# Half of the sigmoids written into PSUM rooms that are taken by need, products shared four to four between VectorE and GpSimd

## Chip, core and metric

The program runs on one core of a Trainium2 chip. The metric is the device time of one execution in microseconds (us). Engines are named as in the profile: PE is TensorE, PEld its weight loads, DVE is VectorE, ACT is ScalarE, POOL is GpSimd, SP issues DMAs.

## The reference

Two layers of attention through 32 inducing points are followed by a feed-forward layer whose activation is a rational function. `h`, which has 49920 rows of 2048 elements, is where the work lies.

```python
def mab(q, kv):
    s = scale * (q @ kv.transpose(0, 2, 1))
    s = s - s.max(-1, keepdims=True)
    a = np.exp(s)
    a /= a.sum(-1, keepdims=True) + 1e-09
    return a @ kv
h = mab(I, x)                       # I: 32 inducing points, x: 4 x 12480 x 128
x = mab(x, h).reshape(49920, 128)
...
h = x @ w_in                        # 49920 x 2048
P = a[0] + a[1]*h + a[2]*h**2 + a[3]*h**3
Q = 1.0 + abs(b[0])*abs(h) + abs(b[1])*h**2
out = (P / (Q + 1e-6)) @ w_out
```

## The kernel before

**Tiling.** The tokens of the four batches are cut into 104 blocks of 480 tokens (26 for each batch). A block has eight *units*, numbered 0 to 7; a unit is 256 of the 2048 hidden columns, held as a tile of 128 partitions x 960 elements. In tile names the three numbers are batch, block and unit (`u1_6_0`). All large instructions come from one recording helper, so that all of them stand on line 157; they are told apart by their tiles.

**A unit's way.** `h` after shifting and scaling is called y here. The rational function is written as a linear part, which one extra matmul adds, and a product of a sum with an inverse; the inverse comes from a logarithm and a sigmoid.

- *first*: two matmuls (PE, `hp<-at,st`) put y into a PSUM tile of two banks, called a *room*. There are three rooms (pool `ps_h`), used in turn as a ring: the room of unit i goes to unit i+3 when the *D* of unit i has read it.
- even units: *mask* (DVE, `u<-hp`) writes |y| into an SBUF tile `u`; *pre* (POOL, `l<-u,all`) writes a scaled copy into the SBUF tile `l`; *D* (DVE, `l<-hp,all,l`) multiplies by y in PSUM. Odd units: *abs* (ACT, `u<-hp,all`) writes `u`; *D* (DVE, `l<-u,all,hp`) follows directly.
- *Ln* (ACT, `u<-u`, 1920 elements, two neighbouring units, called a *pair*) and *sigmoid* (ACT, `u<-u,all`, 1920 elements) turn `u` into the inverse, in place. They lie in different table sets: four pairs of Ln, a table load, four pairs of sigmoid, a table load, and so on.
- the last product, out of `l` and the inverse in `u`: units 0, 1, 3, 5, 7 take it on DVE in one instruction (*Ev*, `l<-l,all,u`, both inputs in SBUF), units 2, 4, 6 on POOL in two (*add*, `l<-l,all`, and *Eg*, `l<-l,u`).
- *second*: four matmul passes (PE, `po<-l,w_out`) add the unit into the block's output in the one `po` bank. After unit 7 *fetch* (DVE, `oT<-po`) copies it out, and a DMA stores it.

**Order.** Each engine executes its instructions in the order in which the program was written. Class `Flow` writes it: it keeps a clock for PE, DVE, ACT and POOL, offers every instruction whose inputs are planned (`options`), takes the one that could start first (ties go by `RANK`, for the attention's own work by `GEN`), books its cost from `COST` and writes it (`do`). The attention work of later blocks and batches is mixed in as generators. The plan has locks: an Ev is not planned to begin while POOL has a product's step running, nor POOL's steps while an Ev runs (`lock_v`, `lock_g`).

SBUF tiles `u` come in 7 pairs (`ROOMS`), tiles `l` in 14 (`SLOTS`). Before the main loop (up to about 87 us of the trace) the first batch's inducing attention and the weights are prepared. A second branch of the program (`general`) is not taken with these inputs.

Of the kernel before, what the change touches and what calls it, by code (L numbers as in the profile page):

```python
# [179 lines left out]
class Flow:  # L180
# [3 lines left out]
    COST = {"first": 0.85, "second": 1.4, "linear": 0.35, "fetch": 0.6, "D": 1.13, "mask": 1.08, "Ev": 1.06, "abs": 0.97, "ln": 1.72, "sig": 1.83, "load": 1.28, "pre": 1.1, "add": 1.15, "Eg": 2.22}  # L184
    BATCH = 4
    ON_POOL = (2, 4, 6)
    ROOMS = 7
    SLOTS = 14
    RANK = {"first": 0, "second": 2, "fetch": 0, "D": 0, "mask": 4, "Ev": -1, "abs": 0, "wide": 1, "pre": 1, "add": 3, "Eg": 2, "load": 1}
    GEN = {"pe": 4, "v": 0, "a": 0, "g": 4, "x": 1}  # L190

    def __init__(self, k, units):
        self.k, self.units = k, units
        self.T = dict.fromkeys(("pe", "v", "a", "g"), 0.0)
        self.now, self.sp = 0.0, 0.0
# [1 line left out]
        self.table, self.nl, self.ns, self.stop = "ln", 0, 0, 0
        self.i1 = self.i2 = self.fetched = 0
        self.masks = self.pres = self.abss = 0
        self.ds, self.es = [], []  # L200
# [39 lines left out]

    def options(self):

        us, LAT, C = self.units, self.LAT, self.COST
        for t in self.turns:
            kind, cost = t.need
            if kind in self.T:
                yield kind, max(t.ready, self.lock_v) if kind == "g" else t.ready, self.GEN[kind], cost, ("turn", t)
            elif kind == "x" and self.table == "ln":
                yield "a", t.ready, self.GEN["x"], cost, ("turn", t)
        if self.i1 < len(us):  # L250
            u, old = us[self.i1], us[self.i1 - 3] if self.i1 >= 3 else None
# [8 lines left out]
        if self.full is not None:  # L260
            yield "v", self.full[1] + LAT, self.RANK["fetch"], C["fetch"], ("fetch", None)
        for u in self.ds:
            s = self.slot_at(u.p)
            if s is not None:
                yield "v", max(u.t["d"], s), self.RANK["D"], C["D"], ("D", u)
        if self.masks < self.pairs:
            u = us[2 * self.masks]
            r = self.room_at(self.masks)
            if "first" in u.t and r is not None:
                yield "v", max(u.t["first"] + LAT, r), self.RANK["mask"], C["mask"], ("mask", u)  # L270
        if self.pres < self.masks:
            u = us[2 * self.pres]
            s = self.slot_at(self.pres)
            if s is not None:
                yield "g", max(u.t["mask"] + LAT, s, self.lock_v), self.RANK["pre"], C["pre"], ("pre", u)
        if self.abss < self.pairs:
            u = us[2 * self.abss + 1]
            r = self.room_at(self.abss)
            if "first" in u.t and r is not None:
                yield "a", max(u.t["first"] + LAT, r), self.RANK["abs"], C["abs"], ("abs", u)  # L280
        for u in [u for u in self.es if not u.pool][:1]:
            yield "v", max(u.t["e"], self.lock_g), self.RANK["Ev"], C["Ev"], ("Ev", u)
        for u in [u for u in self.es if u.pool and self.half is None][:1]:
            yield "g", max(u.t["e"], self.lock_v), self.RANK["add"], C["add"], ("add", u)
        if self.half is not None:
            yield "g", self.lock_v, self.RANK["Eg"], C["Eg"], ("Eg", self.half)
        top = self.stop + self.BATCH
        if self.table == "ln":
            if self.nl < min(top, self.pairs):
                a, b = us[2 * self.nl], us[2 * self.nl + 1]  # L290
                if "D" in b.t and "pre" in a.t and "mask" in a.t:
                    yield "a", max(b.t["D"], a.t["pre"]) + LAT, self.RANK["wide"], C["ln"], ("ln", self.nl)
            elif self.ns < self.pairs:
                yield "a", 0.0, self.RANK["load"], C["load"], ("load", "sig")
# [5 lines left out]
    def room_at(self, p):  # L300

        if p in self.room:
            return 0.0
        if p != len(self.room):
            return None
        if p < self.ROOMS:
            return 0.0
        a, b = self.units[2 * (p - self.ROOMS):][:2]
        return max(a.t["E"], b.t["E"]) + self.LAT if "E" in a.t and "E" in b.t else None

    def slot_at(self, p):

        if p in self.slot:
            return 0.0
        q = 2 * p - self.SLOTS
        if p != len(self.slot):
            return None
        if q < 0:
            return 0.0
        a, b = self.units[q:q + 2]  # L320
        return b.t["second"] + self.LAT if "second" in b.t else None
# [8 lines left out]
    def sums(self, p):  # L330
        k, us = self.k, self.units
        if p not in self.slot:
            self.slot[p] = True
            for u in us[2 * p:2 * p + 2]:
                u.g = k.mp.tile([P, 2, BT], F32, tag="l", name=f"l{u.i}", bufs=self.SLOTS)

    def do(self, what, u, start, end):
# [4 lines left out]
        if what == "turn":  # L342
            u.ready = end + LAT
            if u.need[0] == "g":
                self.lock_g = end
# [3 lines left out]
            return  # L349
        if what == "first":  # L350
            k.first(u)
            u.t["first"] = end + 0.1
# [11 lines left out]
        elif what == "mask":  # L364
            self.pair(self.masks)
            V.tensor_scalar(out=u.u.bitcast(I32), in0=u.h.bitcast(I32), scalar1=0x7FFFFFFF, scalar2=None, op0=ALU.bitwise_and)
            u.t["mask"] = end
            self.masks += 1
        elif what == "pre":
            self.sums(self.pres)  # L370
            G.tensor_scalar(out=u.g, in0=u.u, scalar1=1.0, scalar2=p.k1, op0=ALU.mult, op1=ALU.add)
# [4 lines left out]
        elif what == "abs":
            self.pair(self.abss)
            A.activation(u.u, u.h, AF.Abs, bias=p.back, scale=1.0)
            u.t["d"] = end + LAT
            u.p = self.abss  # L380
            self.ds.append(u)
            self.abss += 1
        elif what == "D":
            if u.key[2] % 2:
                self.sums(u.p)
                V.scalar_tensor_tensor(out=u.g, in0=u.u, scalar=p.k1, in1=u.h, op0=ALU.add, op1=ALU.mult)
            else:
                V.scalar_tensor_tensor(out=u.g, in0=u.h, scalar=p.k2, in1=u.g, op0=ALU.add, op1=ALU.mult)
            u.t["D"] = end
            self.ds.remove(u)  # L390
        elif what == "load":
# [4 lines left out]
        elif what == "ln":
            w = us[2 * u]
            A.activation(w.pair, w.pair, AF.Ln, bias=LAM, scale=LAM)
            self.nl += 1
        elif what == "sig":  # L400
            w = us[2 * u]
            A.activation(w.pair, w.pair, AF.Sigmoid, bias=p.lnc, scale=-2.0)
            for w in us[2 * u:2 * u + 2]:
# [676 lines left out]
```

## Time and profile before

| what | us |
| --- | --- |
| median of 3 runs | 2802.0 (2797.62 to 2804.08) |
| profiled execution, its own time | 2795.03 |
| span of the profiled execution, first to last instruction | 2793.1 |
| busy in the span: DVE / PE / ACT / POOL | 2503.2 / 2275.5 / 2221.1 / 1860.7 |

A row of groups gives the line, engine, operation, the tile written and the tiles read, the shape, the count, then busy time and mean duration of one, then the idle time of the engine just before these instructions and what ended it. "x3" in a timeline stands for three instructions that follow one another, with their common time. Instructions of one engine overlap a little at their ends, so that a run of them takes less than their number times the mean of one.

### The profile page before, as it was taken

The page shows a single profiled execution, that of the slowest core. Times are in us where ns is not written, and L with a number is a line of the kernel's source. Part 1 is how long each engine was busy: PE and PEld are TensorE (multiplying, and loading weights), DVE is VectorE, ACT ScalarE, POOL GpSimd, SP SyncE. Part 2 cuts the span into 40 slices and gives each one's busy share as a digit, 9 for nine tenths or more (in the row PEclk, how much of TensorE's full clock was granted, in tenths as well). Part 3 has the DMA queues.
Part 4 walks back from the last instruction along what each step waited for, and adds up shares of the span by engine and source line. Part 5 has one row for each costly group of instructions (what it writes and reads, how often), then busy time and mean ns, then how long its engine had stood idle before and what let it go on. Part 6 is the DMA issues. An engine that isn't in the chain of part 4 may idle for free.

```text
span 2793.1 us, 23849 instructions
## 1 busy us (share of the span) xinstructions
PE 2275.5 (81%) x7516; PEld 1206.6 (43%) x7516; DVE 2503.2 (90%) x2430; ACT 2221.1 (80%) x1561; POOL 1860.7 (67%) x1212
## 2 busy tenths in 40 slices
PE   5887888887978878878877888878897878777787
PEld 2543444443544434444444444444454444343343
DVE  6688999999899898989999999898999999998996
ACT  1577898887878789877788888888788888778885
POOL 2366667677666676766676766666677767666675
PEclk6689999898989999988999999989999999888898
DMA  8222212111012112211012121221110110000000
GB/s 258 70 58 66 56 44 54 43 53 39 15 60 71 53 39 61 60 26 56 25 43 67 46 59 38 60 54 36 46 32 22 32 39 18 27 20 18 22 14 12
DMA packets 117359, 133.68 MB, mean 48 GB/s; under 512 B 13544, under 2 KB 115816, under 8 KB 117224
## 3 DMA queue, kind: packets, MB, share of 16 engines
q1 hardware_dynamic: 117224, 132.06, 16.8%
q8 instruction: 63, 1.03, 0.2%
q14 instruction: 72, 0.59, 0.1%
HBM read 80.89 MB, written 25.56 MB: 38 GB/s over the span
## 4 chain that ended last, share of the span: by engine, by line
DVE 31%; PE 20%; issue 8%; POOL 4%; ACT 4%; DMA 0%; SPq 0%; DVEq 0%; ACTq 0%; POOLq 0%
DVE l L157 24%; PE po L157 16%; DVE u L157 5%; POOL l L157 4%; PE hp L157 4%; ACT u L157 3%; DVE oT L157 1%; ACT L157 1%; PE pd L157 0%; DVE asm L157 0%; DVE st L157 0%; DMA at<-hl 0%; DVE amx L157 0%; DVE hl L157 0%; DVE gs L157 0%
## 5 line engine op out<-in xcount | busy, mean ns | idle before, releaser
L157 PE MATMUL po<-l,w_out 128*128 128x480 f32 x3328 | 1573.8, 618 | 145.1 <-DVE oT L157 79.0
L157 PEld LDWEIGHTS po<-l,w_out 128*128 128x128 f32 x3328 | 676.2, 208 | 827.4 <-issue 580.7
L157 POOL TENSOR_SCALAR l<-u,all 128x960 f32<-128x960 f32 x416 | 540.3, 1300 | 641.9 <-DVE u L157 538.8
L157 DVE SCALAR_TENSOR_TENSOR l<-l,all,u 128x960 f32<-128x960 f32 x520 | 875.4, 1731 | 14.7 <-ACT u L157 14.4
L157 PE MATMUL hp<-at,st 128*128 128x480 f32 x1664 | 620.9, 478 | 317.1 <-DVE l L157 312.8
L157 POOL TENSOR_TENSOR l<-l,u 128x960 f32<-128x960 f32 x312 | 791.5, 2537 | 125.7 <-ACT u L157 112.3
L157 ACT ACTIVATE u<-u 128x1920 f32<-128x1920 f32 x416 | 733.4, 1799 | 163.2 <-DVE l L157 91.1
L157 ACT ACTIVATE u<-u,all 128x1920 f32<-128x1920 f32 x416 | 769.8, 1891 | 1.0
L157 ACT ACTIVATE u<-hp,all 128x960 f32<-128x960 f32 x416 | 434.6, 1054 | 280.5 <-PE hp L157 247.2
L157 DVE TENSOR_SCALAR u<-hp 128x960 int32<-128x960 int32 x416 | 473.5, 1149 | 115.7 <-PE hp L157 111.1
L157 PEld LDWEIGHTS hp<-at,st 128*128 128x128 f32 x1664 | 308.7, 204 | 580.5 <-issue 300.8
L157 DVE SCALAR_TENSOR_TENSOR l<-u,all,hp 128x960 f32<-128x960 f32 x416 | 495.7, 1203 | 28.9 <-ACT u L157 28.4
L157 DVE SCALAR_TENSOR_TENSOR l<-hp,all,l 128x960 f32<-128x960 f32 x416 | 497.8, 1207 | 24.6 <-POOL l L157 23.7
L157 POOL TENSOR_SCALAR l<-l,all 128x960 f32<-128x960 f32 x312 | 465.6, 1492 | 0.2
L157 ACT ACT_TABLE_LOAD x209 | 268.1, 1283 | 4.4 <-PEq L1073 0.7
L157 PEld LDWEIGHTS pd<-HT,xTb 128*120 128x120 f32 x832 | 105.0, 197 | 17.2 <-issue 14.0
L157 PE MATMUL pd<-HT,xTb 128*120 128x32 f32 x832 | 100.9, 274 | 2.3 <-issue 1.9
L157 DVE COPY oT<-po 128x480 f32<-128x480 f32 x104 | 67.5, 649 | 34.4 <-PE po L157 34.4
L157 PE MATMUL po<-at,st 128*128 128x480 f32 x104 | 78.5, 755 | 0.0
L157 POOL MEMSET x<- 120x4 f32 x104 | 10.5, 113 | 62.9 <-PE ph L157 54.5
L157 PE MATMUL ph<-x,eT 120*32 120x129 f32 x832 | 41.3, 335 | 13.2 <-DMA x<-x_t 10.5
L157 POOL TENSOR_TENSOR st<-gs,st 64x512 fp32r<-64x512 f32 x16 | 20.4, 1277 | 32.8 <-ACT st L157 22.4
(87 smaller groups left out, 595.1 us busy)
## 6 DMA issues: line engine op xcount, KB each, us to landing
x<-x_t SPq DMA_DIRECT2D x104, 240.0 KB, 4.1
xTb<-x_c SPq DMA_DIRECT2D x104, 240.0 KB, 2.9
at<-hl SPq DMA_DIRECT2D x416, 60.0 KB, 2.0
out<-oT SPq DMA_DIRECT2D x104, 240.0 KB, 2.0
xTa<-x_c SPq DMA_DIRECT2D x78, 240.0 KB, 2.9
xTw<-x_c SPq DMA_DIRECT2D x5, 960.0 KB, 11.8
raw<-w_in SPq DMA_DIRECT2D x4, 480.0 KB, 14.0
raw<-w_out SPq DMA_DIRECT2D x5, 384.0 KB, 7.0
```

The costliest lines, as they stand in the source:

```text
L157: ins = call(*args, **kw)
```

## The change

The sigmoid is no longer taken by pairs. Units 0, 2, 4, 6 are now those of DVE: their sigmoid (`sigp`, ACT, 960 elements) is written into a PSUM room, tile `i`, and Ev reads it there (`l<-l,all,i`). Units 1, 3, 5, 7 are those of POOL: their sigmoid (`sig`, ACT, 960 elements) stays in place in `u`, and add and Eg follow on POOL. Which units are masked on DVE (0, 2, 4, 6) and which go through abs on ACT (1, 3, 5, 7) stays as it was.

The three rooms have tags of their own (`hp0` to `hp2`). A first or a sigp takes the room that is free earliest in the plan and holds it until its D or Ev. `u` and `l` are now claimed when the first is planned. The plan's locks are gone, and `RANK`, `GEN` and some of `COST` have other numbers. The dictionary lookups `room_at`, `slot_at`, `pair` and `sums` are replaced by `roomy`, `room` and `slot`, which say the same of `u` and `l` unit by unit; `general_unit` and `misc` name their rooms by tag.

```diff
-    COST = {..., "Ev": 1.06, "abs": 0.97, "ln": 1.72, "sig": 1.83, "load": 1.28, "pre": 1.1, "add": 1.15, "Eg": 2.22}
+    COST = {..., "Ev": 1.13, "abs": 0.97, "ln": 1.72, "sig": 1.83, "half": 0.96, "load": 1.28, "pre": 1.1, "add": 1.13, "Eg": 2.22}
+    RANK = {"first": 1, "second": 2, "fetch": 0, "D": 1, "mask": 2, "Ev": 0, "abs": 1, "wide": 2, "sig": 0, "pre": 0, "add": 2, "Eg": 1, "load": 1}
+    GEN = {"pe": 1, "v": 3, "a": 1, "g": 1, "x": 1}
     BATCH = 4
-    ON_POOL = (2, 4, 6)
     ROOMS = 7
     SLOTS = 14
-    RANK = {"first": 0, "second": 2, "fetch": 0, "D": 0, "mask": 4, "Ev": -1, "abs": 0, "wide": 1, "pre": 1, "add": 3, "Eg": 2, "load": 1}
-    GEN = {"pe": 4, "v": 0, "a": 0, "g": 4, "x": 1}
+    BANKS = 3
+    MASKED = (0, 2, 4, 6)
+    ON_POOL = (1, 3, 5, 7)
...
+    def bank(self):
+        free = [t for t in self.banks if t is not None]
+        return min(free) if free else None
+
+    def take(self):
+        i = self.banks.index(self.bank())
+        self.banks[i] = None
+        return i
...
-        if self.i1 < len(us):
-            u, old = us[self.i1], us[self.i1 - 3] if self.i1 >= 3 else None
+        bank = self.bank()
+        if self.i1 < len(us) and bank is not None and self.roomy(us[self.i1]):
+            u = us[self.i1]
...
-        for u in [u for u in self.es if not u.pool][:1]:
-            yield "v", max(u.t["e"], self.lock_g), self.RANK["Ev"], C["Ev"], ("Ev", u)
+        for u in self.ev[:1]:
+            yield "v", u.t["e"], R["Ev"], C["Ev"], ("Ev", u)
...
-        elif self.ns < self.nl:
-            yield "a", 0.0, self.RANK["wide"], C["sig"], ("sig", self.ns)
+        elif self.sigs:
+            for u in [u for u in self.sigs if u.pool][:1]:
+                if u.n % 2 == 0 and us[u.n + 1].pool:
+                    yield "a", 0.0, R["wide"], C["sig"], ("sig2", u)
+                else:
+                    yield "a", 0.0, R["wide"], C["half"], ("sig", u)
+            for u in [u for u in self.sigs if not u.pool][:1]:
+                if bank is not None:
+                    yield "a", bank, R["sig"], C["half"], ("sigp", u)
...
         elif what == "sig":
-            w = us[2 * u]
-            A.activation(w.pair, w.pair, AF.Sigmoid, bias=p.lnc, scale=-2.0)
+            A.activation(u.u, u.u, AF.Sigmoid, bias=p.lnc, scale=-2.0)
+            u.t["e"] = end + LAT
+            self.sigs.remove(u)
+            self.eg.append(u)
+        elif what == "sigp":
+            u.bank = self.take()
+            u.inv = k.hp(u, "i")
+            A.activation(u.inv, u.u, AF.Sigmoid, bias=p.lnc, scale=-2.0)
+            u.t["e"], u.t["left"] = end + LAT, end
+            self.sigs.remove(u)
+            self.ev.append(u)
         elif what == "Ev":
-            V.scalar_tensor_tensor(out=u.g, in0=u.g, scalar=p.k3, in1=u.u, op0=ALU.add, op1=ALU.mult)
-            u.t["E"] = self.lock_v = end
-            self.es.remove(u)
+            V.scalar_tensor_tensor(out=u.g, in0=u.g, scalar=p.k3, in1=u.inv, op0=ALU.add, op1=ALU.mult)
+            u.t["E"] = end
+            self.banks[u.bank] = end + LAT
+            self.ev.remove(u)
...
+    def hp(self, u, name):
+        return self.ps_h.tile([P, 2, 512], F32, tag=f"hp{u.bank}", name=f"{name}{u.i}", bufs=1)[:, :, 0:BT]
```

ACT's queue from the table load ahead of the sigmoids of block 5 (batch 1) to the last of these sigmoids, before; `u1_6_x` are the abs of the block that follows:

```order
L157 ACT_TABLE_LOAD
L157 ACTIVATE u1_5_0_4827<-u1_5_0_4827,all_202 128x1920
L157 ACTIVATE u1_6_2_4972<-hp1_6_3_4974,all_202 128x960 [waits PE_49]
L157 ACTIVATE u1_5_2_4843<-u1_5_2_4843,all_202 128x1920
L157 ACTIVATE u1_6_4_5008<-hp1_6_5_4991,all_202 128x960 [waits PE_49,Pool_49]
L157 ACTIVATE u1_5_4_4898<-u1_5_4_4898,all_202 128x1920
L157 ACTIVATE u1_5_6_4923<-u1_5_6_4923,all_202 128x1920 [waits Activation_49]
```

The same place after the change; `i1_5_x` are the sigmoids into PSUM rooms:

```order
L157 ACT_TABLE_LOAD
L157 ACTIVATE i1_5_0_5252<-u1_5_0_5084,all_202 128x2x480 [waits DVE_49,PE_49]
L157 ACTIVATE u1_6_0_5216<-h1_6_1_5234,all_202 128x960 [waits PE_49]
L157 ACTIVATE u1_5_0_5084<-u1_5_0_5084,all_202 128x960
L157 ACTIVATE u1_5_2_5111<-u1_5_2_5111,all_202 128x960
L157 ACTIVATE u1_6_2_5242<-h1_6_3_5262,all_202 128x960 [waits PE_49]
L157 ACTIVATE u1_5_4_5157<-u1_5_4_5157,all_202 128x960 [waits Activation_49]
L157 ACTIVATE u1_5_6_5198<-u1_5_6_5198,all_202 128x960 [waits Activation_49]
L157 ACTIVATE i1_5_2_5301<-u1_5_2_5111,all_202 128x2x480 [waits DVE_49]
L157 ACTIVATE u1_6_4_5274<-h1_6_5_5282,all_202 128x960 [waits PE_49,Pool_49]
L157 ACTIVATE i1_5_4_5310<-u1_5_4_5157,all_202 128x2x480 [waits DVE_49]
L157 ACTIVATE i1_5_6_5315<-u1_5_6_5198,all_202 128x2x480 [waits DVE_49]
```

Four instructions of 1920 elements have become eight of 960. The sigmoids into `i` each wait for DVE, which none of the sigmoids did before. The abs of unit 1 of block 6, which stood ahead of this table load, now stands behind it.

DVE's queue at the same place, from the first product of block 5 on, before:

```order
L157 SCALAR_TENSOR_TENSOR l1_5_0_4833<-l1_5_0_4833,all_202,u1_5_0_4827 128x960 [waits Activation_49]
L157 SCALAR_TENSOR_TENSOR l1_5_1_4834<-l1_5_1_4834,all_202,u1_5_0_4827 128x960
L157 SCALAR_TENSOR_TENSOR l1_5_3_4850<-l1_5_3_4850,all_202,u1_5_2_4843 128x960 [waits Activation_49]
L157 SCALAR_TENSOR_TENSOR l1_6_3_4979<-u1_6_2_4972,all_202,hp1_6_3_4974 128x960 [waits PE_49]
L157 TENSOR_SCALAR e2_4361,mxs2_4362<-pc2_4_4994 128x240 [waits PE_49]
L157 SCALAR_TENSOR_TENSOR l1_6_5_5023<-u1_6_4_5008,all_202,hp1_6_5_4991 128x960 [waits Activation_49]
L157 TENSOR_SCALAR e2_4361,mxs2_4362<-pc2_4_4994 128x240
L157 TENSOR_SCALAR u1_6_4_5008<-hp1_6_4_4984 128x960 [waits DVE_49]
L157 TENSOR_SCALAR u1_6_6_5034<-hp1_6_6_5025 128x960 [waits DVE_49,PE_49]
L157 SCALAR_TENSOR_TENSOR l1_5_5_4908<-l1_5_5_4908,all_202,u1_5_4_4898 128x960 [waits Activation_49]
L157 SCALAR_TENSOR_TENSOR l1_5_7_4936<-l1_5_7_4936,all_202,u1_5_6_4923 128x960 [waits Activation_49]
```

And after the change:

```order
L157 SCALAR_TENSOR_TENSOR l1_5_0_5085<-l1_5_0_5085,all_202,i1_5_0_5252 128x960 [waits Activation_49]
L157 COPY oT1_4_5258<-po1_4_0_5175 128x480 [waits DMAHW7_49,PE_49]
L157 SCALAR_TENSOR_TENSOR l1_6_2_5243<-h1_6_2_5244,all_202,l1_6_2_5243 128x960 [waits Pool_49]
L157 SCALAR_TENSOR_TENSOR l1_6_1_5233<-u1_6_0_5216,all_202,h1_6_1_5234 128x960 [waits DVE_49,Activation_49]
L157 SCALAR_TENSOR_TENSOR l1_6_3_5261<-u1_6_2_5242,all_202,h1_6_3_5262 128x960 [waits Activation_49]
L157 TENSOR_SCALAR u1_6_4_5274<-h1_6_4_5276 128x960 [waits PE_49]
L157 SCALAR_TENSOR_TENSOR l1_5_2_5112<-l1_5_2_5112,all_202,i1_5_2_5301 128x960 [waits Activation_49]
L157 SCALAR_TENSOR_TENSOR l1_6_4_5275<-h1_6_4_5276,all_202,l1_6_4_5275 128x960 [waits Pool_49]
L157 SCALAR_TENSOR_TENSOR l1_6_5_5281<-u1_6_4_5274,all_202,h1_6_5_5282 128x960 [waits Activation_49]
L157 SCALAR_TENSOR_TENSOR l1_5_4_5158<-l1_5_4_5158,all_202,i1_5_4_5310 128x960 [waits Activation_49]
L157 SCALAR_TENSOR_TENSOR l1_5_6_5199<-l1_5_6_5199,all_202,i1_5_6_5315 128x960 [waits Activation_49]
```

Five products with two SBUF inputs have become four with one input in PSUM. Between the first and the second of them now stand a fetch, three D and a mask of block 6.

## Rows read from the trace of the kernel before

**Rows 1.** Part 1 of the page: busy us of each engine in the whole span, share, instructions.

```profile
PE 2275.5 (81%) x7516; PEld 1206.6 (43%) x7516; DVE 2503.2 (90%) x2430; ACT 2221.1 (80%) x1561; POOL 1860.7 (67%) x1212
```

**Rows 2.** Busy time of each engine in the stretch from 200 to 2600 us, past the start and ahead of the end.

```profile
core 0: us, PE busy (x) PEld busy (x) DVE busy (x) ACT busy (x) POOL busy (x), PEclk, DMA share, GB/s
200.00:2600.00 2400.00, 1978.94 (x6497) 1054.42 (x6497) 2203.99 (x2000) 1987.52 (x1389) 1655.02 (x1055) 0.91 0.16 43
```

**Rows 3.** Groups of DVE in the same stretch: Ev, the two kinds of D, mask.

```profile
L157 DVE SCALAR_TENSOR_TENSOR l<-l,all,u 128x960 f32<-128x960 f32 x467 | 786.2, 1731 | 9.5 <-ACT u L157 9.2
L157 DVE SCALAR_TENSOR_TENSOR l<-hp,all,l 128x960 f32<-128x960 f32 x373 | 446.3, 1206 | 22.1 <-POOL l L157 21.3
L157 DVE SCALAR_TENSOR_TENSOR l<-u,all,hp 128x960 f32<-128x960 f32 x373 | 444.3, 1203 | 25.1 <-ACT u L157 24.8
L157 DVE TENSOR_SCALAR u<-hp 128x960 int32<-128x960 int32 x374 | 425.6, 1149 | 95.9 <-PE hp L157 91.6 <-issue 1.8 <-POOL l L157 1.2
```

**Rows 4.** Groups of ACT in the same stretch: sigmoid, Ln, abs, table loads.

```profile
L157 ACT ACTIVATE u<-u,all 128x1920 f32<-128x1920 f32 x376 | 696.0, 1891 | 0.9
L157 ACT ACTIVATE u<-u 128x1920 f32<-128x1920 f32 x372 | 655.8, 1799 | 132.8 <-DVE l L157 81.2 <-POOL l L157 44.4 <-DVE asm L157 6.0
L157 ACT ACTIVATE u<-hp,all 128x960 f32<-128x960 f32 x374 | 390.7, 1054 | 258.1 <-PE hp L157 229.9 <-issue 20.5 <-POOL l L157 3.9
L157 ACT ACT_TABLE_LOAD x188 | 241.2, 1283 | 3.3
```

**Rows 5.** Groups of POOL in the same stretch: Eg, pre, add.

```profile
L157 POOL TENSOR_TENSOR l<-l,u 128x960 f32<-128x960 f32 x281 | 709.0, 2523 | 111.0 <-ACT u L157 99.2
L157 POOL TENSOR_SCALAR l<-u,all 128x960 f32<-128x960 f32 x373 | 486.9, 1307 | 560.7 <-DVE u L157 480.3 <-PE po L157 50.3 <-PE hp L157 8.1
L157 POOL TENSOR_SCALAR l<-l,all 128x960 f32<-128x960 f32 x281 | 419.9, 1494 | 0.2
```

**Rows 6.** Least, median and greatest duration in ns over the whole span, of the instructions that write or read the tiles `l` (Ev, the D, pre, add, Eg) and `po`.

```profile
L157 DVE SCALAR_TENSOR_TENSOR l<-l,all,u x520: 1196/1260/3253, 125.3 to 2772.8; 128x960 f32<-128x960 f32 x174
L157 POOL TENSOR_SCALAR l<-u,all x416: 1058/1070/4227, 88.8 to 2758.4; 128x960 f32<-128x960 f32 x139
L157 DVE SCALAR_TENSOR_TENSOR l<-u,all,hp x416: 1119/1204/1216, 90.4 to 2759.1; 128x960 f32<-128x960 f32 x139
L157 DVE SCALAR_TENSOR_TENSOR l<-hp,all,l x416: 1125/1206/1220, 92.0 to 2760.3; 128x960 f32<-128x960 f32 x139
L157 POOL TENSOR_SCALAR l<-l,all x312: 1058/1078/4414, 123.8 to 2774.9; 128x960 f32<-128x960 f32 x156
L157 POOL TENSOR_TENSOR l<-l,u x312: 2207/2250/4540, 127.7 to 2777.0; 128x960 f32<-128x960 f32 x156
```

**Rows 7.** The timeline of DVE and of POOL near 1530 us: start and length in us, engine, operation, tiles, count; in brackets the idle time ahead and its releaser.

```profile
1520.20 2.34 DVE L157 SCALAR_TENSOR_TENSOR l<-u,all,hp 128x960 f32<-128x960 f32 x2 [0.50 <-ACT u L157]
...
1523.59 7.36 DVE L157 SCALAR_TENSOR_TENSOR l<-l,all,u 128x960 f32<-128x960 f32 x4
...
1535.89 1.21 DVE L157 SCALAR_TENSOR_TENSOR l<-l,all,u 128x960 f32<-128x960 f32 x1
...
1520.86 1.07 POOL L157 TENSOR_SCALAR l<-l,all 128x960 f32<-128x960 f32 x1
1524.84 3.16 POOL L157 TENSOR_TENSOR l<-l,u 128x960 f32<-128x960 f32 x1 [2.92 <-ACT u L157]
1527.99 1.96 POOL L157 TENSOR_SCALAR l<-l,all 128x960 f32<-128x960 f32 x1
...
1536.14 1.89 POOL L157 TENSOR_SCALAR l<-u,all 128x960 f32<-128x960 f32 x1 [0.59 <-PE po L157]
```

**Rows 8.** The timeline of ACT at the same place: two abs in a row, then three sigmoids in a row.

```profile
1519.11 2.01 ACT L157 ACTIVATE u<-hp,all 128x960 f32<-128x960 f32 x2
1521.01 5.47 ACT L157 ACTIVATE u<-u,all 128x1920 f32<-128x1920 f32 x3
```

**Rows 9.** Waits over the whole span: engine and tile, what it waited for, us in total, times, longest.

```profile
PE hp L157 <- DVE l L157: 312.8, 221, 8.9
...
ACT u L157 <- PE hp L157: 247.2, 119, 6.6
PEld hp L157 <- DVE l L157: 200.3, 176, 7.1
```

**Rows 10.** Part 4 of the page: shares of the span in the chain of work that ended last, by engine and by line.

```profile
DVE 31%; PE 20%; issue 8%; POOL 4%; ACT 4%; DMA 0%; SPq 0%; DVEq 0%; ACTq 0%; POOLq 0%
```

**Rows 11.** Second matmuls over the whole span (least, median, greatest ns; first and last start), and two runs of them in the timeline.

```profile
L157 PE MATMUL po<-l,w_out x3328: 563/566/1169, 126.6 to 2787.2; 128*128 128x480 f32 x196
...
1518.80 3.38 PE L157 MATMUL po<-l,w_out 128*128 128x480 f32 x8
1531.57 8.49 PE L157 MATMUL po<-l,w_out 128*128 128x480 f32 x16 [5.43 <-DVE oT L157]
```

More of the change, by code (lines that the diff above doesn't have):

```diff
@@ L194, in __init__ @@
         self.T = dict.fromkeys(("pe", "v", "a", "g"), 0.0)
-        self.now, self.sp = 0.0, 0.0
+        self.now, self.sp, self.free_at = 0.0, 0.0, 0.0
         self.turns, self.holder = [], None
[L197 to L200, printed above, removed]
+        self.table, self.nl, self.stop = "ln", 0, 0
+        self.i1 = self.i2 = 0
+        self.masks, self.pres, self.abss, self.ds, self.sigs, self.ev, self.eg = [], [], [], [], [], [], []
         self.pairs = len(units) // 2
-        self.room, self.slot = {}, {}
-        self.po_end, self.full = 0.0, None
-        self.lock_v, self.lock_g, self.half = 0.0, 0.0, None
+        self.banks = [0.0] * self.BANKS
+        self.po_end, self.full, self.half = 0.0, None, None
+        self.log = []
+        for i, u in enumerate(units):
+            u.n, u.masked, u.pool = i, u.key[2] in self.MASKED, u.key[2] in self.ON_POOL
     def issue(self, cost):
@@ L260, in options @@
+            if "E" in u.t and (u.key[2] or self.full is None) and (not last or "linear" in self.k.ready_cols[u.key[0]]):
+                yield "pe", max(u.t["E"] + LAT, self.po_end if u.key[2] == 0 else 0.0), R["second"], C["second"] + C["linear"] * last, ("second", u)
         if self.full is not None:
-            yield "v", self.full[1] + LAT, self.RANK["fetch"], C["fetch"], ("fetch", None)
+            yield "v", self.full[1] + LAT, R["fetch"], C["fetch"], ("fetch", None)
         for u in self.ds:
-            s = self.slot_at(u.p)
@@ L264, in options @@
[L264 to L280, printed above, removed]
-        for u in [u for u in self.es if not u.pool][:1]:
-            yield "v", max(u.t["e"], self.lock_g), self.RANK["Ev"], C["Ev"], ("Ev", u)
-        for u in [u for u in self.es if u.pool and self.half is None][:1]:
-            yield "g", max(u.t["e"], self.lock_v), self.RANK["add"], C["add"], ("add", u)
+            yield "v", u.t["d"], R["D"], C["D"], ("D", u)
@@ new lines, in options @@
+        for u in self.masks[:1]:
+            yield "v", max(u.t["first"] + LAT, self.room(u)), R["mask"], C["mask"], ("mask", u)
+        for u in self.pres[:1]:
+            yield "g", max(u.t["mask"] + LAT, self.slot(u)), R["pre"], C["pre"], ("pre", u)
+        for u in self.abss[:1]:
+            yield "a", max(u.t["first"] + LAT, self.room(u)), R["abs"], C["abs"], ("abs", u)
+        for u in self.ev[:1]:
+            yield "v", u.t["e"], R["Ev"], C["Ev"], ("Ev", u)
+        for u in self.eg[:1]:
+            if self.half is None:
+                yield "g", u.t["e"], R["add"], C["add"], ("add", u)
@@ L285, in options @@
         if self.half is not None:
-            yield "g", self.lock_v, self.RANK["Eg"], C["Eg"], ("Eg", self.half)
-        top = self.stop + self.BATCH
+            yield "g", 0.0, R["Eg"], C["Eg"], ("Eg", self.half)
         if self.table == "ln":
[L289 to L294, printed above, removed]
-        elif self.ns < self.nl:
-            yield "a", 0.0, self.RANK["wide"], C["sig"], ("sig", self.ns)
-        elif self.nl < self.pairs:
-            yield "a", 0.0, self.RANK["load"], C["load"], ("load", "ln")
@@ L300, in room_at @@
[L300 to L321, printed above, removed]
@@ L395, in do @@
                 self.stop = self.nl
+            else:
+                self.sigs = us[2 * self.stop:2 * self.nl]
         elif what == "ln":
@@ L906, in shifted @@
     def shifted(self, q):
[L908 removed]
+        return self.fast and q not in Flow.MASKED
+    def hp(self, u, name):
+        return self.ps_h.tile([P, 2, 512], F32, tag=f"hp{u.bank}", name=f"{name}{u.i}", bufs=1)[:, :, 0:BT]
     def first(self, u):
```

112 lines of the change are left out of this document (58 added, 54 removed).

## The prediction

> **What bounds the kernel now.** Read the engines' busy times first. Over the span DVE is busy for 90%, PE 81%, ACT 80%, POOL 67% [rows 1], so DVE is the first suspect, with three others not far behind. The start differs from the rest, so I work with the steady stretch of 2400 us. It holds 374 masks [rows 3], four for a block: 93.5 blocks, 25.67 us each. For one block DVE is busy 2203.99/93.5 = 23.57 us (91.8%), ACT 21.26, PE 21.16, POOL 17.70 [rows 2]. The chain that ended last names the same two engines in front, DVE 31% and PE 20% [rows 10]. The waits say how DVE holds the others: a first waits for its room until a D on DVE has read it (312.8 and 200.3 us, PE's two queues), and then abs on ACT waits for that first (247.2 us) [rows 9].
>
> Next, what DVE's time is made of. Ev takes 1731 ns in the mean, the two D, of the same shape and operation, 1203 and 1206 [rows 3]. Ev's median is 1260 and its least 1196, but its greatest is 3253; no D takes over 1220 [rows 6]. The timeline tells why. Four Ev in a row take 7.36 us, 1.84 each, and in that time a POOL Eg takes 3.16 and an add 1.96; where an Ev begins first and takes its 1.21 us, it is the pre beside it that takes 1.89, and an add with no Ev beside it takes 1.07 [rows 7]. So Ev, with both inputs in SBUF, and POOL's instructions stop each other. A D, with one input in PSUM, is not stopped although POOL works for 69% of that stretch.
>
> **Ev part by part.** The change takes one Ev in five from DVE and lets the other four read PSUM. The new form (`l` from SBUF, the inverse from PSUM) is not in the trace; its nearest row is the D with the inputs the same way (`l<-u,all,hp`), 1.19 us of busy time each in a row (444.3/373) [rows 3]. Bounds: 1.12, the shortest D, and 1.68, Ev as it is now (786.2/467). I take 1.20, since a PSUM input is what separates the rows that stretch from those that don't. For a block: 786.2/93.5 = 8.41 us now, 4 x 1.20 = 4.80 after; DVE falls from 23.57 to 19.96 (19.6 to 21.9 with the bounds). [...]
>
> **Sigmoids.** Four instructions of 1920 elements become eight of 960. Three long ones in a row take 5.47 us, 1.82 each; two abs of 960 in a row take 2.01, 1.005 each [rows 8]. A half sigmoid lies between 0.91 (half of a long one) and 1.054 (a lone abs, [rows 4]); whether writing to PSUM costs more no row shows, and the abs, which crosses between the memories the other way, is the nearest. At 1.005 the eight take 8.04 us where 696.0/93.5 = 7.44 are spent now: ACT goes from 21.26 to 21.86 (21.1 to 22.3). The count of table loads, Ln and abs stays.
>
> **POOL.** One add and one Eg more for a block, and the stretching goes. Medians are 1.070 (pre), 1.078 (add), 2.250 (Eg) [rows 6]: 4 x 4.398 = 17.59 us against (709.0 + 486.9 + 419.9)/93.5 = 17.28 now [rows 5]; POOL goes from 17.70 to 18.0. That work lies beside ACT's and comes before the seconds of odd units; nothing but `po` waits for it, and 18.0 of some 24 leaves room. With no gain from the contention it would be 21.7.
>
> **PE.** Its instructions stay the same, 21.16 us a block at the granted clock of 0.91 [rows 2]; eight seconds in a row take 3.38 us in one place and sixteen take 8.49 in another, just after an idle time of 5.43 us [rows 11]. So shorter waits may give some of it back; I count nothing.
>
> **Who bounds then.** ACT, with 21.86, ahead of PE 21.16, DVE 19.96, POOL 18.0. What it has to wait for is new: a sigmoid into PSUM waits for a room, and behind it on ACT stand the abs of the next block and the next Ln phase. Walk the list of ACT after the change. The `i` of unit 2 takes 1.0 us, its Ev on DVE 1.2; ACT fills that with one abs, and the third `i` finds the rooms taken by units 4 and 5 of the next block and by the second `i`: about 0.4 us of waiting. The fourth waits about 0.2 for the D of unit 4. At the end of the Ln phase the last Ln needs the D of units 6 and 7, whose firsts come behind all that: about 0.7. That is 1.3, a period of 23.2 us, with everything else in time. The other way to set it: if ACT gets as full as DVE is now, 21.86/0.918 = 23.8. Since PE is then closer behind than any engine is behind DVE now, I take **24.0**.
>
> The time: 104 blocks x 25.67 = 2669.7 us of the span of 2793.1 leave 123.4 for the start and the end; the first second begins at 126.6 [rows 11]. 104 x 24.0 + 123.4 = 2619.4; the profiled execution's own time is 1.9 above its span (2795.03), and the median of the runs 7.0 above that: **2628 us**. In the same way each period below becomes a time: 104 x period + 132.3.
>
> **Rivals.**
> - *As full as it can be*: only the walk's waits and less, a period of 22.4 to 23.2, 2462 to 2545 us. For: DVE gets slack of 4 us a block, so that D and Ev come at once. Against: no engine is over 92% full now. 0.14.
> - *Rooms are short*: three rooms now serve 8 firsts for a block, then 12 holds. If each of the four `i` waits 0.35 us beyond the above, the period is 25.4: 2774 us. For: firsts wait for rooms already, 513 us in all [rows 9], and the order puts three D and a mask between two Ev, each of which gives back a room. Against: most of today's wait is for a DVE that is 92% full. [...] 0.15.
> - *Stretching stays*: Ev from PSUM is still stopped by POOL. DVE 21.9, POOL 21.7, ACT 21.9, PE 21.2, all alike, a period near 25.0: 2732 us. Against: the D [rows 6]. 0.05.
> - *Slower*: ACT's idle time isn't DVE's load but the loop first, abs, D, room. ACT idles 25.67 - 21.26 = 4.41 us a block, of which the abs lose 258.1/93.5 = 2.76 and Ln 1.42 [rows 4]. If these stay because the rooms freed by a quicker D are taken by `i`, the period is 21.86 + 4.41 = 26.27: 2864 us. It is slower from an idle time of 3.8 us a block on. For: all of ACT's waits run through rooms. Against: the D that they wait for come 15% denser in a DVE with slack. 0.12.
>
> **How the numbers follow.** The forecast (period 23.2 to 24.7, 2545 to 2701 us) has 0.50, the rivals 0.14, 0.15, 0.05 and 0.12, no change 0.04 (a measurement here can tell 0.2%, about 6 us). The likeliest gives 2628. The range reaches from 2514 (22.9; half of the first rival below it) to 2784 (25.5; all of the slower case, no change and a little of the short rooms above it). Faster: 0.50 + 0.14 + 0.15 + 0.05 = 0.84; same 0.04; slower 0.12.
>
> **What would show it.** Right: Ev (`l<-l,all,i`) with a mean of 1.15 to 1.25 us and no long ones, DVE near 2130 us, pre, add and Eg with means near 1.07, 1.08 and 2.25, the half sigmoids near 1.05 alone, ACT near 2285 us busy and the fullest engine of the steady stretch, at over 90%, with its waits split between PE's firsts and DVE's rooms. Wrong: Ev over 1.4 us or Eg over 2.4 (stretching stays); sigmoids waiting on DVE for over 150 us, with ACT under 87% full (rooms); abs still waiting for firsts for over 200 us (slower). A half sigmoid into PSUM of over 1.15 us would add 0.4 us a block and more.

## The result and the profile after

The changed kernel takes 2487.47 us in the median of 4 runs (2483.85 to 2493.28), beside 2799.81 us before: a ratio of 0.8885, 95% interval 0.8863 to 0.8907. I had forecast 2628 us and a range from 2514, so the direction held and the gain came out nearly twice as large, past the low end of the range. The profiled execution took 2483.85 us, its span 2482.0.

Part 1 of the page, and from part 2 the clock that PE was granted in 40 slices, in tenths of full speed:

```profile
PE 2149.5 (87%) x7516; PEld 1145.8 (46%) x7516; DVE 2124.4 (86%) x2326; ACT 2283.7 (92%) x1977; POOL 1877.0 (76%) x1420
...
PEclk6699999999999999999999999999999999999999
```

ACT is now the fullest engine and DVE has lost 379 us of busy time [rows 1]. PE ran the same 7516 matmuls in 126 us less.

The steady stretch, as in [rows 2]:

```profile
200.00:2300.00 2100.00, 1859.10 (x6432) 992.46 (x6432) 1847.70 (x1889) 2024.30 (x1747) 1658.43 (x1233) 0.96 0.18 49
```

It holds 372 masks, 93.0 blocks of 22.58 us. For one block ACT is busy 21.77 us (96.4%), PE 19.99, DVE 19.87, POOL 17.83.

Groups of DVE, of ACT and of POOL in that stretch, which answer to [rows 3 to 5]:

```profile
L157 DVE SCALAR_TENSOR_TENSOR l<-u,all,h 128x960 f32<-128x960 f32 x371 | 446.6, 1207 | 82.2 <-ACT u L157 81.0
L157 DVE SCALAR_TENSOR_TENSOR l<-l,all,i 128x960 f32<-128x960 f32 x370 | 439.6, 1207 | 40.3 <-ACT i L157 39.0
L157 DVE TENSOR_SCALAR u<-h 128x960 int32<-128x960 int32 x372 | 426.9, 1150 | 62.3 <-PE h L157 55.4 <-PE pm L157 3.9 <-POOL l L157 2.2
```

```profile
L157 ACT ACTIVATE u<-u 128x1920 f32<-128x1920 f32 x372 | 656.0, 1798 | 16.2 <-DVE l L157 15.4
L157 ACT ACTIVATE u<-h,all 128x960 f32<-128x960 f32 x371 | 387.7, 1050 | 24.9 <-PE h L157 22.0 <-POOL l L157 1.1 <-PE pt L157 0.6
L157 ACT ACTIVATE u<-u,all 128x960 f32<-128x960 f32 x370 | 387.6, 1087 | 0.0
L157 ACT ACTIVATE i<-u,all 128x960 f32<-128x960 f32 x369 | 385.7, 1059 | 30.1 <-DVE l L157 28.0
```

```profile
L157 POOL TENSOR_TENSOR l<-l,u 128x960 f32<-128x960 f32 x371 | 832.1, 2243 | 138.4 <-ACT u L157 119.8
L157 POOL TENSOR_SCALAR l<-l,all 128x960 f32<-128x960 f32 x371 | 398.1, 1073 | 0.4
L157 POOL TENSOR_SCALAR l<-u,all 128x960 f32<-128x960 f32 x371 | 397.7, 1073 | 268.1 <-DVE u L157 247.9 <-DVE nmc L157 9.3 <-ACT i L157 5.2
```

The reader should see two things. Ev (`l<-l,all,i`) has the duration of a D, 1207 ns, and pre, add and Eg have means of 1073, 1073 and 2243 ns, near their medians of before [rows 6]. And in the last column ACT hardly waits: 30.1 us for rooms (`i`), 24.9 ahead of abs (258.1 before), 16.2 ahead of Ln (132.8 before).

Least, median and greatest duration of add, Eg and Ev over the span, beside [rows 6]: the long ones, up to 3253 and 4540 ns, are gone.

```profile
L157 POOL TENSOR_SCALAR l<-l,all x416: 1056/1072/1235, 121.4 to 2470.8; 128x960 f32<-128x960 f32 x139
L157 POOL TENSOR_TENSOR l<-l,u x416: 2209/2240/2429, 122.5 to 2472.0; 128x960 f32<-128x960 f32 x139
L157 DVE SCALAR_TENSOR_TENSOR l<-l,all,i x416: 1194/1206/1216, 123.5 to 2461.8; 128x960 f32<-128x960 f32 x139
```

The chain that ended last, shares of the span (DVE led it with 31% before, [rows 10]):

```profile
ACT 44%; PE 20%; DVE 20%; issue 9%; POOL 5%; DMA 2%; SPq 0%; ACTq 0%; DVEq 0%; POOLq 0%
```

### The profile page after: what moved, and what is told of

It reads as the page before. It is cut to its first block, busy times and chain, and to the rows that moved or that the text cites. A ratio compares the mean times of both kernels' runs of the same rounds, so it can differ in the third digit from the quotient of the medians.

```text
span 2482.0 us, 24331 instructions
## 1 busy us (share of the span) xinstructions
PE 2149.5 (87%) x7516; PEld 1145.8 (46%) x7516; DVE 2124.4 (86%) x2326; ACT 2283.7 (92%) x1977; POOL 1877.0 (76%) x1420
## 3 DMA queue, kind: packets, MB, share of 16 engines
q8 instruction: 63, 1.03, 0.2%
## 4 chain that ended last, share of the span: by engine, by line
ACT 44%; PE 20%; DVE 20%; issue 9%; POOL 5%; DMA 2%; SPq 0%; ACTq 0%; DVEq 0%; POOLq 0%
ACT u L157 30%; DVE l L157 14%; PE po L157 13%; ACT i L157 8%; ACT L157 5%; POOL l L157 5%; PE h L157 4%; DVE u L157 3%; PE pd L157 1%; DVE oT L157 1%; DMA x<-x_t 1%; PE ph L157 0%; DMA raw<-w_in 0%; DVE asm L157 0%; DMA xTw<-x_c 0%
## 5 line engine op out<-in xcount | busy, mean ns | idle before, releaser
L157 POOL TENSOR_TENSOR l<-l,u 128x960 f32<-128x960 f32 x416 | 932.7, 2242 | 162.3 <-ACT u L157 141.6
L157 PE MATMUL h<-at,st 128*128 128x480 f32 x1664 | 664.0, 491 | 130.5 <-DVE l L157 125.9
L157 ACT ACTIVATE u<-u 128x1920 f32<-128x1920 f32 x416 | 733.8, 1798 | 25.8 <-DVE l L157 24.9
L157 DVE SCALAR_TENSOR_TENSOR l<-u,all,h 128x960 f32<-128x960 f32 x416 | 501.0, 1207 | 94.6 <-ACT u L157 93.4
L157 DVE SCALAR_TENSOR_TENSOR l<-h,all,l 128x960 f32<-128x960 f32 x416 | 501.8, 1210 | 63.6 <-POOL l L157 60.9
L157 DVE TENSOR_SCALAR u<-h 128x960 int32<-128x960 int32 x416 | 477.5, 1150 | 79.7 <-PE h L157 72.8
L157 DVE SCALAR_TENSOR_TENSOR l<-l,all,i 128x960 f32<-128x960 f32 x416 | 493.8, 1207 | 45.4 <-ACT i L157 44.1
L157 PEld LDWEIGHTS h<-at,st 128*128 128x128 f32 x1664 | 294.1, 193 | 445.3 <-issue 220.9
L157 ACT ACTIVATE i<-u,all 128x960 f32<-128x960 f32 x416 | 434.3, 1058 | 34.7 <-DVE l L157 32.4
L157 ACT ACTIVATE u<-h,all 128x960 f32<-128x960 f32 x416 | 434.9, 1051 | 32.9 <-PE h L157 29.9
L157 POOL TENSOR_SCALAR l<-l,all 128x960 f32<-128x960 f32 x416 | 446.3, 1073 | 0.4
L157 ACT ACTIVATE u<-u,all 128x960 f32<-128x960 f32 x416 | 435.5, 1087 | 0.0
```

The costliest lines, as they stand in the source:

```text
L157: ins = call(*args, **kw)
```

## The experiments

Each run stands beside its own runs of the kernel before; "a block" is the steady stretch divided by its masks. Period, DVE and ACT are us for one block; the last column is the engine with the largest share of that stretch. A period is good to about 0.1 us, since one mask more or less in the stretch already moves it by 0.06.

| run | median us | ratio to before (95%) | period | DVE | ACT | fullest engine |
| --- | --- | --- | --- | --- | --- | --- |
| before | 2799.81 | 1 | 25.67 | 23.57 | 21.26 | DVE 91.8% |
| changed kernel | 2487.47 | 0.8885 (0.8863 to 0.8907) | 22.58 | 19.87 | 21.77 | ACT 96.4% |
| e1 in place | 2741.96 | 0.9787 (0.9765 to 0.9809) | 25.07 | 22.65 | 21.90 | DVE 90.3% |
| e9 in place, locks | 2756.18 | 0.9846 (0.9825 to 0.9867) | 25.34 | 22.55 | 21.98 | DVE 89.0% |
| e2 ring | 2717.61 | 0.9713 (0.9696 to 0.9730) | 24.93 | 20.24 | 21.99 | ACT 88.2% |
| e3 five and three | 2545.08 | 0.9098 (0.9081 to 0.9114) | 23.31 | 20.90 | 21.92 | ACT 94.1% |
| e4 wrong costs | 2548.11 | 0.9099 (0.9082 to 0.9117) | 23.31 | 20.00 | 21.94 | ACT 94.1% |
| e5 two masks twice | 2638.94 | 0.9423 (0.9397 to 0.9448) | 24.06 | 22.19 | 21.93 | DVE 92.2% |
| e13 all masks twice | 2859.67 | 1.0233 (1.0200 to 1.0266) | 26.18 | 24.31 | 22.12 | DVE 92.9% |
| e10 first twice | 2504.98 | 0.8949 (0.8929 to 0.8968) | 22.83 | 20.10 | 21.90 | ACT 95.9% |
| e7 five masked | 2489.23 | 0.8888 (0.8862 to 0.8915) | 22.78 | 20.99 | 21.06 | ACT 92.5% |
| e6 pairs | 2469.83 | 0.8816 (0.8787 to 0.8846) | 22.52 | 19.93 | 21.48 | ACT 95.4% |
| e15 pairs, PE costs | 2449.42 | 0.8777 (0.8742 to 0.8811) | 22.34 | 19.82 | 21.43 | ACT 95.9% |
| e14 pairs in front | 2491.35 | 0.8912 (0.8881 to 0.8943) | 22.76 | 19.97 | 21.56 | ACT 94.7% |
| e11 pairs, batch of 5 | 2651.80 | 0.9468 (0.9446 to 0.9490) | 24.26 | 20.07 | 21.07 | ACT 86.9% |
| e12 pairs, batch of 6 | 2850.84 | 1.0182 (1.0160 to 1.0204) | 26.30 | 20.19 | 20.86 | ACT 79.3% |
| e8 before, mean costs, no locks | 2995.83 | 1.0698 (1.0668 to 1.0728) | 27.51 | 25.48 | 21.25 | DVE 92.6% |

**Was it the stretching?** e1 keeps the order on every engine, instruction for instruction, and moves only the place of one result. The tile `u` is then held until Ev has read it.

```diff
         elif what == "sigp":
             u.bank = self.take()
-            u.inv = k.hp(u, "i")
+            u.inv = u.u
...
-            u.t["e"], u.t["left"] = end + LAT, end
+            u.t["e"] = end + LAT
...
-            u.t["E"] = end
+            u.t["E"] = u.t["left"] = end
```

> The changed kernel with the order of every engine word for word the same, but the sigmoids of DVE's units are written in place into u (SBUF) and their Ev reads u; no sigmoid uses a PSUM room. Theory A (the gain comes from VectorE and GpSimd no longer stopping each other): Ev goes back to a mean of 1.55 to 1.8 us with a greatest of over 3, pre, add and Eg to means near 1.3, 1.5 and 2.5, DVE to 22 us a block, and the period from 22.6 to 25 or more: 2650 to 2800 us. Rival B (the gain comes from the rooms by need, the split and the new order, all of which stay here): within 1% of 2487, 2465 to 2515 us.

Measured: 2741.96 us, as theory A said; rival B falls. Ev in the stretch from 200 to 2500 us of this run, then three rows of its tile `l` (least, median, greatest):

```profile
L157 DVE SCALAR_TENSOR_TENSOR l<-l,all,u 128x960 f32<-128x960 f32 x365 | 681.7, 1886 | 21.4 <-ACT u L157 20.8
...
L157 POOL TENSOR_SCALAR l<-l,all x416: 1058/1076/3167, 121.4 to 2728.4; 128x960 f32<-128x960 f32 x139
L157 POOL TENSOR_TENSOR l<-l,u x416: 2207/2243/3267, 122.5 to 2729.5; 128x960 f32<-128x960 f32 x139
L157 DVE SCALAR_TENSOR_TENSOR l<-l,all,u x416: 1196/1938/3233, 123.6 to 2718.4; 128x960 f32<-128x960 f32 x139
```

The medians of POOL are the clean ones, the greatest are stretched again, and half of the Ev take over 1.9 us; their mean, 1886 ns, is a little above what theory A named. The longer hold of `u` is not behind it: masks and abs, which write `u` next, wait in that stretch for at most 2.5 us in all that an Ev could have ended. One operand's place is worth 254 us, 81% of the whole gain of 312. Could a plan avoid the overlaps instead? e9 gives e1 the locks of the kernel before; one of the changed lines:

```diff
-            yield "v", u.t["e"], R["Ev"], C["Ev"], ("Ev", u)
+            yield "v", max(u.t["e"], self.lock_g), R["Ev"], C["Ev"], ("Ev", u)
```

> The run with the sigmoids in place (e1_in_place, 2742 us), planned with the locks of the kernel before, so that an Ev and a step of POOL are not planned to overlap. If the stretching can be planned away: Ev back to a mean under 1.5 us and 2500 to 2560 us, near the changed kernel. If it can't, since POOL's 17.8 us and four Ev of 1.2 that may not overlap fill 22.6 us of a block by themselves: 2640 us or over, whatever Ev's mean is.

Measured: 2756.18 us, Ev at 1853 ns in the mean: these locks did not plan the stretching away. That it is so because POOL's steps and Ev must share the block's time was argued, not shown. For the kernel before, e8 took its locks out and told the plan the mean durations of the trace.

```diff
-    COST = {..., "Ev": 1.06, ..., "pre": 1.1, "add": 1.15, "Eg": 2.22}
+    COST = {..., "Ev": 1.68, ..., "pre": 1.3, "add": 1.49, "Eg": 2.52}
...
-            yield "v", max(u.t["e"], self.lock_g), self.RANK["Ev"], C["Ev"], ("Ev", u)
+            yield "v", u.t["e"], self.RANK["Ev"], C["Ev"], ("Ev", u)
```

> The kernel before, planned without the locks and with the mean durations of its own trace (Ev 1.68, pre 1.30, add 1.49, Eg 2.52 us). Nothing is taken from the stretching. If a plan that is told nearer durations was a large part of the gain: 2700 to 2760 us. If the kernel before was held by the stretched Ev whatever the plan says: within 1% of 2800, 2772 to 2828 us.

Both expectations missed: 2995.83 us, 7% slower, with Ev at 2081 ns in the mean (1731 before). Means without locks made a worse order than locks with short costs; which of the two changes did it was not looked at apart.

**Do the rooms have to be taken by need?** e2 hands them out in a ring.

```diff
     def bank(self):
-        free = [t for t in self.banks if t is not None]
-        return min(free) if free else None
+        return self.banks[self.turn3]
...
-        i = self.banks.index(self.bank())
+        i = self.turn3
+        self.turn3 = (i + 1) % self.BANKS
```

> The changed kernel, but the three PSUM rooms are handed out in a ring to firsts and sigmoids in the order in which they are planned, not by which is free first. If rooms are not what ACT waits for (theory A): at most 1% more than 2487, up to 2512 us, ACT still over 94% full in the steady stretch. Rival B (taking rooms by need is a part of the gain): at least 2% more, 2537 us or over, with PE's firsts and the sigmoids into PSUM waiting for DVE for over 150 us more than now (245 and 32 us).

Measured: 2717.61 us; the rival holds in the time, and by more than it said. Three groups of ACT in this run from 200 to 2500 us:

```profile
L157 ACT ACTIVATE u<-u 128x1920 f32<-128x1920 f32 x370 | 647.8, 1796 | 16.8 <-POOL l L157 11.8 <-DVE l L157 4.4
L157 ACT ACTIVATE i<-u,all 128x960 f32<-128x960 f32 x372 | 388.4, 1058 | 170.8 <-DVE l L157 166.8 <-PE po L157 2.6
...
L157 ACT ACTIVATE u<-h,all 128x960 f32<-128x960 f32 x368 | 382.9, 1051 | 77.9 <-PE h L157 74.4 <-POOL l L157 2.8
```

Ev stays clean in this run (1208 ns), and the time is lost ahead of `i`: 170.8 us beside 30.1. The other half of the rival's sign missed: over the span the firsts waited 205.8 us for DVE, less than the 244.9 of the changed kernel. A hold by a masked unit (first, mask, pre, D) lasts longer than one by a sigmoid (sigmoid, Ev): 6.64 and 2.78 us in the median of the changed kernel's steady stretch. That in a ring the short wait behind the long fits this, but the ring also changes the order of the plan, and the two were not taken apart. The two parts of the change are not additive: without the PSUM operand 254 us of the gain go, without rooms by need 230.

**The split.** e3 gives POOL three units again.

```diff
-    ON_POOL = (1, 3, 5, 7)
+    ON_POOL = (2, 4, 6)
```

> The changed kernel with the split of before: POOL has units 2, 4, 6 and DVE the five others, each through a PSUM room. By the sum of work DVE goes from 19.87 to 21.07 us a block and POOL from 17.83 to 14.5; ACT stays at 21.77. If DVE's slack is what keeps ACT full: a period of 22.9 to 23.4 and 2505 to 2555 us. If the split does not matter: 2480 to 2495 us. If POOL's own length is what held things up: under 2475 us.

Measured: 2545.08 us, period 23.31, in the range that DVE's slack called for: 1.03 us more on DVE cost 0.73 us by the periods and 0.55 by the medians (57.6/104), though ACT does the same work and POOL less. The run also gives POOL other units, and such a choice alone can move 1% (e14 beside e6).

**How full can the busiest engine get?** This is the term that I got wrong. e4 plans with the durations of the kernel before (`"Ev": 1.73`, `"pre": 1.3`, `"add": 1.49`, `"Eg": 2.52`).

> The changed kernel planned with the durations that the kernel before had (Ev 1.73, pre 1.30, add 1.49, Eg 2.52 us) while the real ones stay what they are, so that only the order changes. If my forecast was too long because a plan that tells the true durations leaves few waits: a plan told wrong ones costs 2% or more, 2537 us or over. If it is the engines' slack that leaves few waits, whatever the plan was told: within 1%, 2465 to 2512 us.

Measured: 2548.11 us: the same durations on the chip, 2.4% lost by the order alone, 61 of the 140.5 us by which the forecast was too long. e5 doubles the mask of two units, e13 of all four, planned at twice the cost.

```diff
...
-            V.tensor_scalar(out=u.u.bitcast(I32), in0=u.h.bitcast(I32), scalar1=0x7FFFFFFF, ...)
+            for _ in range(1 + (u.key[2] in (0, 4))):
                 V.tensor_scalar(out=u.u.bitcast(I32), in0=u.h.bitcast(I32), scalar1=0x7FFFFFFF, ...)
```

> The changed kernel with the mask of units 0 and 4 done twice (same values) and planned so: 2.1 us more of DVE for a block, from 19.87 to 22.0, as full as ACT with 21.77; no stretching, and a plan that knows it. If a true plan alone keeps the busiest engine at 95% or more: a period of at most 23.2 and up to 2552 us. If two engines of the same load cost each other waits (the slack theory, and the share of 92% that my forecast used): a period of 23.8 or more, 2614 us and over.

> The changed kernel with every mask done twice (same values) and planned so: DVE goes to 24.1 us a block, the fullest engine by 2.3 us over ACT (21.8), as in the kernel before (23.57 and 21.26), but with nothing stretched. If the fullest engine loses 8% wherever it is DVE: a period near 26.2, 2860 us. If the kernel before lost its 8% to stretching that no plan can place, and a fullest engine with slack beside it gets to 96%: a period near 25.1, 2750 us.

Measured: 2638.94 and 2859.67 us, both on the side of the lost 8%. The steady stretch of e13, 200 to 2700 us, and its masks and Ev:

```profile
200.00:2700.00 2500.00, 2032.84 (x6571) 1080.98 (x6571) 2321.56 (x2325) 2112.51 (x1796) 1703.31 (x1266) 0.88 0.15 42
```

```profile
L157 DVE TENSOR_SCALAR u<-h 128x960 int32<-128x960 int32 x764 | 879.8, 1154 | 115.9 <-PE h L157 101.6
...
L157 DVE SCALAR_TENSOR_TENSOR l<-l,all,i 128x960 f32<-128x960 f32 x381 | 446.9, 1204 | 0.8 <-ACT i L157 0.6
```

Nothing is stretched (Ev takes 1204 ns in the mean, the D 1204 and 1209, and POOL 17.84 us a block beside 17.83 in the changed kernel), DVE is 2.2 us ahead of ACT (2.3 in the kernel before), and it gets to 92.9%, beside 91.8% there. What it waits for is a first, 101.6 us, as in [rows 3] (91.6). One order of causes fits: the first waits for a room that only a D or an Ev on DVE frees, so DVE waits for itself by way of PE. This is argued, not shown: the second mask also lengthens the hold of a masked unit's room, from 6.64 to 8.09 us in the median, and no run without stretching makes DVE the fullest in another way. e10 loads PE instead, and plans it so.

```diff
-        for k in range(2):
+        for k in (0, 1, 0, 1) if self.fast and q in (0, 4) else (0, 1):
```

> The changed kernel with the two matmuls of the first of units 0 and 4 done twice (same values) and planned so: some 1.1 us more of PE for a block, from 20.0 to 21.1, what I had counted for PE in the forecast. If a PE close behind ACT costs ACT waits, as the choice of 24.0 said: a period of 23.2 or more, 2552 us and over. If not: at most 22.8, up to 2510 us, with ACT over 95% full.

Measured: 2504.98 us. The steady stretch of e10, which holds 368 masks:

```profile
200.00:2300.00 2100.00, 1924.68 (x6773) 1054.14 (x6772) 1849.60 (x1879) 2014.69 (x1735) 1647.09 (x1225) 0.96 0.18 48
```

PE is at 20.92 us a block (1924.68/92.0), ACT at 95.9%: 0.93 us more of PE cost 0.17 us a block by the medians (17.5/104), so a PE close behind cost little here.

**A faster version.** e7 masks a fifth unit on DVE (`MASKED = (0, 2, 4, 6, 7)`), e6 pairs POOL's units so that their sigmoids are long again (`ON_POOL = (2, 3, 6, 7)`).

> The changed kernel with unit 7 masked on DVE too, so that three abs are left for ACT. For a block ACT falls to 20.8 us, DVE rises to 20.9, POOL to 18.9, PE stays near 20.0. If ACT's length alone sets the period: 21.6 us and 2385 us. If slack beside the busiest engine is needed: DVE and ACT, now alike, lose what ACT gains, a period of 22.3 to 22.9, 2460 to 2520 us.

> The changed kernel with POOL's units paired, 2, 3, 6, 7 in place of 1, 3, 5, 7: their sigmoids are two instructions of 1920 elements instead of four of 960. Two halves in a row take 1.98 us, a long one 1.82: ACT falls by about 0.35 us a block to 21.4. If ACT's own length sets the period: 22.2 us and 2445 to 2460 us. Rival: two units of POOL in a row come late for their second matmuls and hold u longer: 2487 us or more.

e7 measured 2489.23 us, no gain: ACT fell by 0.7 us and DVE rose by 1.1, and the fullest engine stops at 92.5%. e6 measured 2469.83 us, between its two expectations: ACT 0.29 us shorter, of which 0.17 arrived by the medians (17.6/104); the interval of its ratio lies clear of the changed kernel's. From e6 I went three ways: other pairs (e14, units 0, 1, 4, 5), longer batches (`BATCH` 5 and 6), and PE's costs nearer to the trace (e15).

> The run with POOL's units in pairs (e6_pairs, 2470 us), with units 0, 1, 4, 5 on POOL in place of 2, 3, 6, 7. The same work on every engine; if the order of the units in a block does not matter, 2460 to 2480 us; if POOL's pairs, which take longest, do better in front of DVE's: under 2455 us.

e14 measured 2491.35 us, which neither case had: with the same work on every engine the order of the units moves 1%, and to the worse.

> The run with POOL's units in pairs (e6_pairs, 2470 us) with batches of five pairs of Ln and sigmoid between table loads, in place of four: a fifth of the table loads less, 0.51 us of ACT for a block. If ACT's length sets the period: 2415 to 2430 us. Rival: with five of seven u pairs in a batch the next firsts find no u: 2470 us or over.

> The same with batches of six pairs: a third of the table loads less, 0.86 us of ACT for a block. If ACT's length sets the period: 2380 to 2395 us. Rival: with six of seven u pairs in a batch the next firsts find no u: 2470 us or over, and slower than with five.

The batches measured 2651.80 and 2850.84 us. The table loads went as counted, but the rival held: ACT's wait for DVE ahead of Ln grew to 169.5 us and 331.2 us (15.4 in the changed kernel), in stretches in which DVE's D waited 103.7 and 208.1 us for POOL (53.3); that the want of free `u` is behind it was not looked at apart.

```diff
-    COST = {"first": 0.85, "second": 1.4, ...}
+    COST = {"first": 0.6, "second": 1.62, ...}
```

> The run with POOL's units in pairs (e6_pairs, 2470 us), planned with costs of PE nearer to its trace: first 0.6 in place of 0.85 us, second 1.62 in place of 1.4. If what the plan is told still costs waits at 95%: 2440 to 2460 us; if not: within 0.5% of 2470.

Measured: 2449.42 us, a ratio of 0.8777 (0.8742 to 0.8811), the lowest here and 1.2% below the changed kernel's. Its interval overlaps that of e6, so it is not shown that the costs of PE made e6 faster.

## Why the prediction was wrong, point by point

- *What bounds the kernel*: DVE, by Ev and POOL stopping each other. Right; e1 shows it, for 254 of the 312 us, with the order of every engine kept.
- *Ev part by part*: 1.20 us taken, 1.19 measured (439.6/370); DVE 19.96 forecast, 19.87 measured. The shortest Ev takes 1194 ns with the inverse in PSUM; before, with it in SBUF, it took 1196 [rows 6].
- *Sigmoids*: ACT 21.86 forecast, 21.77 measured. Into PSUM a half takes 1059 ns, in place 1087. In a row the two follow each other 0.99 us apart alike, so the 28 ns between them buy no throughput.
- *POOL*: 18.0 forecast, 17.83 measured.
- *PE*: "I count nothing". The term was mis-sized: 19.99 instead of 21.16, with the granted clock of the stretch at 0.96 instead of 0.91. It explains little of the miss, as e10 shows, where PE was nearly that long again (20.92) and the time 2504.98 us.
- *Who bounds then*: ACT, right, and the signs that I had named for being right came in with it (DVE 2124.4 us, ACT 2283.7); of ACT's idle time they asked no more than a share of over 90%. **The step that failed is the last one: "if ACT gets as full as DVE is now, 21.86/0.918 = 23.8. Since PE is then closer behind than any engine is behind DVE now, I take 24.0".** The share does not pass from one engine to another. DVE as the fullest engine stood at 89 to 93%, with stretching (e9, e1, before, e8) and without (e5, e13). ACT with DVE 1.9 us behind stood at 96%, and at 79 to 94% where batches, rooms, split or order were worse (e12, e11, e2, e3, e4), so that it has no share of its own either. And the addition for PE was wrong (e10). Why DVE stops at 93% stays open; e13's waits only suggest it. The period was 22.58; 1.42 us a block is 148 us, while start and end took 133.7 us instead of 123.4 by the same sum.
- *The walk* gave 23.2, nearer than what I chose over it. It named the right waits but made them too long: 0.6 us for rooms became 0.32 (30.1/93.0), 0.7 ahead of the last Ln became 0.17. Ahead of the abs, where it had none, 0.27 were lost.
- *Rivals*: "as full as it can" came in, at 0.14; against it I had set that no engine was over 92% full, which is the same error. "Slower" had ACT's idle time stay; it fell from 4.41 us to 0.81, and the firsts' waits for DVE from 513 us to 245. "Stretching stays" fell: no Ev takes over 1216 ns. "Rooms are short" is a real cost in a ring (e2, 170.8 us of waiting ahead of `i`) that is small in the changed kernel, which takes rooms by need (30.1 us).

## What to carry to other kernels

A share of busy time is a result of the waits in one order of one kernel, and not a property to carry along (ACT, as the fullest engine, stood at 79 to 96% in these runs): when the bound moves to another engine, walk the new engine's queue instead of carrying the old share over. When two engines stretch each other's instructions, look for the operand that makes them meet; moving one into another memory was worth 254 us here, with the order unchanged. Where buffers are held for unequal times, as the rooms here (6.64 and 2.78 us), try taking them by need: the ring took 230 us more (e2), with another order as well. A plan's costs are worth keeping true where the durations are steady: 2.4% here (e4). Where two engines stretch each other, mean durations were no help (e8, 7% slower, without the locks as well).

## What the runs showed of the chip that I had not expected

PE's time moved with its neighbours. With the same matmuls in the steady stretch's blocks it was busy 21.16 us a block at a granted clock of 0.91 before and 19.99 at 0.96 after; in e13 the clock was 0.88 and PE took 21.29 (2032.84/95.5). These are means over stretches at full and at half clock: in the kernel before, the matmuls of second took 566 ns in the median from 1500 to 1510 us, where the granted clock was 1.00, and 1007 ns from 1528.5 to 1535 us, where it was 0.50. That shorter waits raise the clock is read from these rows and was not tested by itself. A gain on another engine thus came with a second one on PE, which my sum left out; it was worth little here, where ACT sets the period.
